# First layer norm of three segments applied to the input's turned copy, with its scales and offsets spread through DRAM

## The chip, the cores and the metric

The kernel runs on one core of one Trainium2 chip. A core has TensorE (PE in the profile; PEld its weight loads), VectorE (DVE), ScalarE (ACT), GpSimd (POOL) and SyncE (SP), each with an instruction queue of its own, and 16 DMA engines that move data between DRAM and the on-chip memory. The metric is the device time of one execution in microseconds; the median of the runs counts.

## The reference

The input x has 2048 tokens of 1024 channels. One block of attention with a compressive memory and one MLP follow each other, both behind a layer norm without weights:

```python
def _layernorm(x, axis=-1, eps=1e-5):
    m = jnp.mean(x, axis=axis, keepdims=True)
    v = jnp.var(x, axis=axis, keepdims=True)
    return (x - m) / jnp.sqrt(v + eps)

# _A_ref(x, wq, wk, wv, wo, beta): H = 32 heads of Dh = 32, N = 4 segments of L = 512 tokens
#   q, k, v = x @ wq, x @ wk, x @ wv, cut into heads and segments
#   for each segment s:
#     p = softmax(q k^T / sqrt(Dh) + causal mask);  a_dot = p v
#     a_mem = (phi(q) M) / (phi(q) z + 1e-6);  phi(t) = t + 1 for t > 0, exp(t) otherwise
#     o = g a_mem + (1 - g) a_dot;  M += phi(k)^T v;  z += sum phi(k)
#   return o @ wo
h = x + _A_ref(_layernorm(x), A_wq, A_wk, A_wv, A_wo, A_beta)
h2 = h + (gelu(_layernorm(h) @ w1 + b1) @ w2 + b2)      # d_ff = 3584
```

## The kernel before

The tokens are worked off in two halves of 1024 (`HT`), each of two segments of 512 tokens. A segment is named (half, sl), with sl 0 or 1. A half passes through attention, the output projection, the second layer norm and the first MLP product ("mixer pairs", 14 in a half); the second MLP product closes the kernel. Float32 precision is reached on TensorE with split operands: each operand is held as a high part and a low part, and `mm3` issues three products (high by high, high by low, low by high).

**What the first norm has to deliver.** The projections need the normalised segment turned, with channels on the partitions: `yh` and `yl`, high and low part, of 8 blocks of 128 channels by 512 tokens. Before the change every segment but the very first goes through `ln1`: four tiles of 128 tokens by 1024 channels are loaded (`xt`). VectorE takes the statistics of each (`bn_stats` L134, `bn_aggr` L138). GpSimd makes the scale and the offset, one number for each token and so for each partition (L141, L142, L147). ACT normalises the tile (L182). `ln_transpose` then turns it with TensorE, in two groups of four transposes of 128x128 (L161) into one PSUM bank; ACT copies the bank out as the high part (L163), and VectorE subtracts that for the low part (L165). A segment has 8 such groups. Segment (0,0) is done by `opening`, which the change leaves alone.

**Where the norms run.** `ln1` is a generator, which its caller advances step by step between other work:
- Segment (0,1) is normalised inside the attention of half 0, during units 0 and 1. A unit is a group of four heads in one segment, and has 24 steps; a step is one `mm3` of a projection (k, q, v: `kps`, `qps`, `vps`) and what `at(step, ...)` has put on it. A variable `acc` grows by 0.7 at each step, and each time it reaches 1 the generator is advanced once.
- Segment (1,0) is normalised during the last nine mixer pairs of half 0, by `interleave(pairs, norms, 0.17)`: 0.17 steps of the norm for each step of the pairs. The tiles of (1,1) are loaded there too.
- The rest of segment (1,1), `acts["ahead"]`, is done in units 0 and 1 of half 1, at 0.55 for each step.

**What sets the order.** The recorded instructions stand in program order on each engine; an engine takes its own queue in order and waits at the head of it. SyncE starts nearly all DMAs. A unit's products reach attention through it: a projection is corrected on VectorE (`side` and `kk`, `qq`, L443), and SyncE copies its rows in three DMAs for each of four groups into `ks` and `qs` (L420). TensorE then forms scores `pqk` from them (L563), VectorE reduces these with the mask (L565), ACT takes the exponential sum (L567, `junk`), and a score block frees the PSUM buffer for another. Weights for the next group of heads are loaded by SyncE (`wr`, L682) and split by VectorE (L689) and GpSimd (L693, four pieces for each weight). In unit 0 of each half GpSimd also writes the mask and a pattern `pat` (L341 to L357), which VectorE casts into `ks` (L676).

Of the kernel before, what the change touches and what calls it, by code (L numbers as in the profile page):

```python
# [10 lines left out]
F32 = mybir.dt.float32  # L11
F32R = mybir.dt.float32r
AF = mybir.ActivationFunctionType
ALU = mybir.AluOpType
# [3 lines left out]
P = 128  # L18
S = 2048
D = 1024  # L20
# [7 lines left out]
HT = 1024  # L28
# [12 lines left out]
EPS = 1e-5  # L41
# [6 lines left out]
def raw(ap):  # L48
    return ap.bitcast(F32)


def build(tc, x, wq, wk, wv, wo, beta, w1, b1, w2, b2, out):
# [16 lines left out]
    mhalf = const.tile([P, 1], F32, name="mhalf")  # L69
# [27 lines left out]
    acts = {}  # L97
# [107 lines left out]
    def chain(*gens):  # L205
        for g in gens:
            yield from g
# [6 lines left out]
    def ln1(half, sl, delay=0, aside=None, gap=1):  # L214
        xs = []
        for t in range(4):
            xt = lnp.tile([P, D], F32, tag="ln", name="xt", bufs=4)
            r0 = half * HT + (4 * sl + t) * P
            nc.sync.dma_start(xt, x[0, r0:r0 + P, :])
            xs.append(xt)  # L220
        for _ in range(delay):
            yield

        def home():
            if ("y", half, sl) not in acts:
                acts["y", half, sl] = acts["y", sl] = seg_tiles(sl, "y")
            return acts["y", sl]

        yield from ln_tiles(lnp, xs, None, None, False, act=True, aside=aside, gap=gap,
                            fold=lambda src, t4: ln_transpose(src, *home(), t4, ("av", "pt", "pt"), slow=True))  # L230

    def opening():

# [129 lines left out]
    def attention(half, first):  # L363
# [343 lines left out]
            at(6, partial(wsplit, 0, "v", "scalar", 6))  # L707
        for m, f in first.pop("rest").items() if first else ():
            at(m, f)
        side = acts.pop("ahead") if half else ln1(0, 1, 3, gap=2)  # L710
        if first:
            next(side)
        for n in range(16):
            u = unit(n)
            heads(u, 24 * n)
            g, sl = ORDER[n]
# [26 lines left out]
            acc = 0.0  # L743
            for c in range(24):
                name = "kqv"[c // 8]
# [685 lines left out]

    for half in range(2):
        acts["zt"] = zt = tc.alloc_tile_pool(name=f"zt{half}", bufs=1, side="right")
        attention_pool(half)
        first = None if half else opening()
        if half:
# [11 lines left out]
        if half == 0:  # L1448
            nc.sync.dma_start(mz_dram, acts["mz"])
        ab.release()  # L1450
        zx = acts["zx"] = tc.alloc_tile_pool(name=f"zx{half}", bufs=1, side="right", reuse_waits="tile")
        mq = tc.alloc_tile_pool(name=f"mq{half}", bufs=1, side="right", reuse_waits="tile")
        pp = tc.alloc_tile_pool(name=f"post{half}", bufs=1, reuse_waits="tile")
# [93 lines left out]
    top.close()  # L1547


_INS = ["A_x", "A_wq", "A_wk", "A_wv", "A_wo", "A_beta", "B_w1", "B_b1", "B_w2", "B_b2"]  # L1550


# [16 lines left out]
```

## Time and profile before

| | |
|---|---|
| median of the runs | 2188.95 us (3 runs, 2188.53 to 2190.12) |
| profiled execution | 2189.65 us, its span 2187.9 us |
| mean granted TensorE clock | 0.999 |
| TensorE busy | 2159.1 us, 99% of the span |
| VectorE, ACT, GpSimd busy | 1363.0, 1100.8, 949.9 us |
| transposes of the first norm by `ln_transpose` | 96, the first at 32.1 us, the last at 878.5 us |

All rows of the prediction come from this profiled execution. A row of a timeline has the start in us, the duration in us, the engine, the line, the operation, what it writes and reads, the shape, and in brackets the idle time of the engine just before and what ended it. A row of the stretches has the window, its length, the busy time (and number of instructions) of PE, PEld, DVE, ACT and POOL, the granted clock, the DMA share and GB/s. A row of grouped instructions has the line, the operation, the count, and smallest, median and largest duration in ns. A row of DMA issues has the count, the size of each and the median time from issue to landing.

### The profile page before, as it was taken

Reading aid. Unit: us, or ns where it says so; the run is one execution under the profiler, and the core shown is the slowest. Engines: PE = TensorE matmul, PEld = TensorE weight load, DVE = VectorE, ACT = ScalarE, POOL = GpSimd, SP = SyncE. Lnnn points to the kernel's source line nnn. Section 1 sums busy time; section 2 is a strip of 40 time slices with the busy share of each in tenths; the row PEclk is TensorE's granted clock in tenths of the full one; section 3 lists DMA queues with packets and bytes.
Section 4 is the critical chain, followed back from the end, with each engine's and each line's share of the span. In section 5 each row is a group of like instructions: output and inputs, shape, how many; then the busy total and the mean of one; then the engine's idle time right before and its main releaser. Section 6 shows DMA issues by size and latency. Waiting matters only on the chain.

```text
span 2187.9 us, 33209 instructions
## 1 busy us (share of the span) xinstructions
PE 2159.1 (99%) x10937; PEld 1750.7 (80%) x10937; DVE 1363.0 (62%) x2696; ACT 1100.8 (50%) x2433; POOL 949.9 (43%) x1206
## 2 busy tenths in 40 slices
PE   7999999999999999999999999999999999999999
PEld 6777777778888887877777768888887888888887
DVE  6766666665745656766667655745666765577653
ACT  5777777762543445777777652643443232323221
POOL 5533335562444434433335561534445544256330
PEclk9999999999999999999999999999999999999999
DMA  6544445664575655544444664575569775576762
GB/s 181 136 107 106 106 106 136 192 199 164 156 209 155 183 163 138 139 108 108 107 108 131 197 192 147 173 217 161 171 189 378 270 231 187 190 245 229 247 223 92
DMA packets 352405, 376.20 MB, mean 172 GB/s; under 512 B 27214, under 2 KB 244330, under 8 KB 352234
## 3 DMA queue, kind: packets, MB, share of 16 engines
q1 hardware_dynamic: 288778, 336.98, 50.8%
q10 hardware_dynamic: 63456, 37.10, 5.6%
q8 instruction: 87, 1.43, 0.3%
q14 instruction: 84, 0.69, 0.1%
HBM read 241.27 MB, written 82.38 MB: 148 GB/s over the span
## 4 chain that ended last, share of the span: by engine, by line
PE 89%; DMA 4%; DVE 3%; ACT 1%; POOL 1%; issue 1%; SPq 0%; ACTq 0%; DVEq 0%; POOLq 0%
PE po L1405 22%; PE bps L1009 10%; PE cps L1009 7%; PE dps L1009 6%; PE pst L613 3%; PE po L627 3%; PE pqk L563 3%; PE kps L127 3%; PE pwo L127 3%; PE kps L128 3%; PE qps L127 2%; PE kps L129 2%; PE pwo L129 2%; PE pwo L128 2%; PE qps L128 2%; PE qps L129 2%
## 5 line engine op out<-in xcount | busy, mean ns | idle before, releaser
L565 DVE CUSTOM_DVE_ANT_0 pqk<-pqk,mask 128x512 f32<-128x512 f32 (+2 forms) x384 | 216.9, 565 | 241.3 <-PE pqk L563 214.8
L567 ACT ACTIVATE junk<-pqk,mx 128x512 f32<-128x512 f32 (+2 forms) x384 | 225.1, 586 | 137.1 <-DVE mx L565 130.5
L620 POOL TENSOR_SCALAR_AFFINE_SELECT e<-e 128x128 f32<-128x128 f32 (+1 forms) x384 | 136.2, 356 | 268.3 <-ACT e L616 254.5
L693 POOL TENSOR_TENSOR wl<-wr,wh 128x256 fp32r<-128x256 f32 x268 | 198.5, 756 | 112.1 <-PE pqk L563 88.1
L616 ACT ACTIVATE e<-pst 128x384 f32<-128x384 f32 (+1 forms) x384 | 200.3, 528 | 72.3 <-PE pst L613 70.3
L1415 DVE TENSOR_TENSOR c<-c,po 128x512 f32<-128x512 f32 x160 | 105.4, 683 | 152.4 <-PE po L1405 149.6
L563 PE MATMUL pqk<-ks,qs 96*128 96x512 f32 (+2 forms) x384 | 138.8, 362 | 7.1 <-DMA qs<-qq 4.3
L613 PE MATMUL pst<-qs,ks 104*128 104x512 f32 (+3 forms) x512 | 140.9, 318 | 1.0 <-ACT e L616 0.4
L613 PEld LDWEIGHTS pst<-qs,ks 104*128 104x128 f32 x512 | 95.7, 188 | 34.7 <-ACT e L616 10.7
L1405 PE MATMUL po<-w2h,zh 128*128 128x512 f32 x378 | 121.0, 390 | 0.7 <-DVE zh L1345 0.4
L1262 POOL TENSOR_TENSOR w2r<-w2r 128x512 f32<-128x512 f32 x54 | 85.9, 1603 | 73.7 <-DMA w2r<-in_B_w 50.0
L127 PE MATMUL qps<-yh,wh 128*128 128x512 f32 x256 | 113.8, 444 | 0.0
L127 PE MATMUL kps<-yh,wh 128*128 128x512 f32 (+1 forms) x264 | 113.0, 428 | 0.0
L1009 PE MATMUL bps<-zh,sb 128*128 128x512 f32 x336 | 111.1, 391 | 0.0
L1009 PE MATMUL bps<-zh,sa 128*128 128x512 f32 x336 | 110.8, 390 | 0.0
L1121 POOL TENSOR_TENSOR s<-r 128x512 f32<-128x512 f32 x28 | 44.1, 1575 | 143.4 <-DVE sa L1137 84.9
L127 PE MATMUL vps<-yh,wh 128*128 128x512 f32 x256 | 105.0, 410 | 0.0
L1405 PE MATMUL po<-w2h,hl 128*128 128x512 f32 x322 | 103.1, 390 | 0.4 <-DVE hl L1345 0.3
L128 PE MATMUL kps<-yl,wh 128*128 128x512 f32 (+1 forms) x264 | 102.4, 388 | 0.9 <-DVE yl L289 0.5
L129 PE MATMUL kps<-yh,wl 128*128 128x512 f32 (+1 forms) x264 | 101.8, 386 | 0.0
L128 PE MATMUL qps<-yl,wh 128*128 128x512 f32 x256 | 101.4, 396 | 0.0
L129 PE MATMUL qps<-yh,wl 128*128 128x512 f32 x256 | 101.0, 394 | 0.0
(271 smaller groups left out, 6211.1 us busy)
## 6 DMA issues: line engine op xcount, KB each, us to landing
hr<-h_dram SPq DMA_DIRECT2D x112, 448.0 KB, 5.4
w2r<-in_B_w SPq DMA_DIRECT2D x122, 256.0 KB, 4.4
r<-in_B_w SPq DMA_DIRECT2D x56, 512.0 KB, 4.7
ks<-kk SPq DMA_DIRECT2D x360, 64.0 KB, 2.0
qs<-qq SPq DMA_DIRECT2D x360, 64.0 KB, 2.0
h_dram<-ht ACTq DMA_DIRECT2D x84, 256.0 KB, 3.7
wx<-in_B_w SPq DMA_DIRECT2D x56, 256.0 KB, 3.5
o_dram<-side SPq DMA_DIRECT2D x52, 256.0 KB, 3.9
```

Of the source, the lines that this page charges most:

```text
L127: nc.tensor.matmul(ps, ah, bh, start=first, stop=False)
L128: nc.tensor.matmul(ps, ah, bl, start=False, stop=False)
L129: acts["mm"] = nc.tensor.matmul(ps, al, bh, start=False, stop=last)
L563: nc.tensor.matmul(ps, u["qs"][0:96, j, i * P:(i + 1) * P], u["ks"][0:96, j, 0:n], start=True, stop=True)
L565: nc.vector.tensor_tensor_reduce(out=ps, in0=ps, in1=mask[:, 512 - n:512], op0=ALU.add, op1=ALU.min, scale=-SCALE, scalar=3.0e38, accum_out=m)
L567: at(now[0] + 1, lambda: nc.scalar.activation(acts["junk"][:, :n], ps, AF.Exp, bias=m, scale=-1.0, accum_out=u["mx"][:, 1, i, j:j + 1]))
L613: nc.tensor.matmul(ps[:, o:o + 512 - P * jk], u["ks"][:, j, jk * P:(jk + 1) * P], u["qs"][:, j, jk * P:512], start=True, stop=True)
L616: nc.scalar.activation(e, ps[:, :w], AF.Exp, scale=SCALE)
L620: nc.gpsimd.affine_select(d, d, pattern=[[0, 2], [1, P]] if n == 2 else [[1, P]], compare_op=ALU.is_ge, fill=0.0, base=0, channel_multipli ...
L693: nc.gpsimd.tensor_tensor(l[:, c], wr[:, c], raw(h)[:, c], op=ALU.subtract)
L1009: nc.tensor.matmul(ps, x_[:, c, :], y_[:, c, :], start=first and c == 0 and n == 0, stop=last and c == 3 and n == 2, skip_group_check=True)
L1405: nc.tensor.matmul(ps, x_[:, k], y_[k], start=opens and k == 0 and i == 0, stop=closes and k == self.KP - 1 and i == 2, skip_group_check=True)
```

## The change

A second input is made on the host before the launch: `A_xT`, the transpose of x, 1024 by 2048. For the segments (0,1), (1,0) and (1,1), `ln1` is replaced by two generators.

`row_scales` still loads the four tiles of x and takes their statistics. GpSimd writes scale and offset of the tokens into one tile `rn` of 128 partitions by 8 numbers, and one DMA stores it, turned, to `rn_dram` (8 by 128).

`column_pairs` loads the segment from the turned input, in four tiles `xc` of 128 partitions by 2 by 512 (512 KB each), and loads `rn_dram` spread over all 128 partitions as `rows` (scales and offsets of 512 tokens, 512 KB in the on-chip memory). Then VectorE multiplies each `xc` by the scales, GpSimd adds the offsets, ACT copies the high part, and VectorE subtracts it for the low part, each on 128x1024. No transposes are left in these segments. The generator is advanced at 0.9 instead of 0.7 for each step in half 0, 0.23 instead of 0.17 in the mixer pairs; the 0.55 of half 1 stays. A pool for `rn` and `rows` is new. The changed kernel's lines are 1 to 65 further down than before (L443 is L502, L563 is L622, L565 is L624, L676 is L735, L689 is L748, L693 is L752).

```diff
+    rn_dram = {k: dram.tile([8, P], F32, name=f"rn_dram{k[0]}{k[1]}") for k in ((0, 1), (1, 0), (1, 1))}
...
+    def row_scales(half, sl):
+        rn = acts["rnp"].tile([P, 8], F32, name="rn", bufs=2)
+        xs = []
+        for t in range(4):
+            xt = lnp.tile([P, D], F32, tag="ln", name="xt", bufs=4)
+            r0 = half * HT + (4 * sl + t) * P
+            nc.sync.dma_start(xt, x[0, r0:r0 + P, :])
+            xs.append(xt)
+        for _ in range(3):
+            yield
+        for t in range(4):
...
+            r = rn[:, t:t + 1]
+            nc.gpsimd.tensor_scalar(v[:, 0:1], mv[:, 1:2], 1.0, EPS, op0=ALU.mult, op1=ALU.add)
+            nc.gpsimd.tensor_tensor(r, v[:, 0:1], mhalf, op=ALU.pow)
+            nc.gpsimd.tensor_scalar(rn[:, 4 + t:5 + t], mv[:, 0:1], -1.0, r, op0=ALU.mult, op1=ALU.mult)
+            yield
+        nc.sync.dma_start(rn_dram[half, sl].rearrange("k p -> p k"), rn)
+        yield
+
+    def column_pairs(half, sl):
+        t0 = half * HT + 512 * sl
+        ws = []
+        for c in range(4):
+            w = lnp.tile([P, 2, 512], F32, tag="ln", name="xc", bufs=4)
+            nc.sync.dma_start(w, xt_[256 * c:256 * c + 256, t0:t0 + 512].rearrange("(c p) n -> p c n", p=P))
+            ws.append(w)
+            if c % 2:
+                yield
+        rows = acts["rnp"].tile([P, 2, 512], F32, name="rows", bufs=1)
+        nc.sync.dma_start(rows.rearrange("p a n -> p (a n)"),
+                          rn_dram[half, sl].rearrange("k p -> (k p)").partition_broadcast(P))
+        for _ in range(2 if half else 3):
+            yield
+        r, nb = (rows[:, i, :].unsqueeze(1).to_broadcast([P, 2, 512]) for i in range(2))
+        home = []
+        for c in range(5):
+            if c < 4:
+                nc.vector.tensor_tensor(ws[c], ws[c], r, op=ALU.mult)
+                nc.gpsimd.tensor_tensor(ws[c], ws[c], nb, op=ALU.add)
+                yield
+            if c > 0:
...
+                home.append(nc.scalar.copy(yh[:, k, :], ws[c - 1]))
+                yield
+                nc.vector.tensor_tensor(yl[:, k, :], ws[c - 1], raw(yh[:, k, :]), op=ALU.subtract)
+                yield
...
-        side = acts.pop("ahead") if half else ln1(0, 1, 3, gap=2)
+        side = acts.pop("ahead") if half else chain(row_scales(0, 1), column_pairs(0, 1))
...
-                    acc += 0.55 if half else 0.7
+                    acc += 0.55 if half else 0.9
...
-            acts["ahead"] = ln1(1, 1, gap=2)
+            acts["rnp"] = tc.alloc_tile_pool(name="rn1", bufs=1, reuse_waits="tile")
+            acts["ahead"] = column_pairs(1, 1)
             interleave(chain(*(mixer.pair(j) for j in range(HP - 9, HP))),
-                       chain(ln1(1, 0, 2), islice(acts["ahead"], 3)), 0.17)
+                       chain(row_scales(1, 0), column_pairs(1, 0), row_scales(1, 1), islice(acts["ahead"], 3)), 0.23)
```

How the rows now stand is shown at three places: in two queues of half 0's units 0 and 1, and in one of half 1's. First SyncE's queue in unit 0 of half 0, before:

```order
L420 DMA ks_179<-side 32x512 x6
L682 DMA wr<-in_A_wk 128x8x128
L420 DMA qs_181<-side 32x512 x3
L682 DMA wr<-in_A_wq 128x8x128
L420 DMA ks_179<-side 32x512 x3
L420 DMA qs_181<-side 32x512 x3
```

The same place after, where the six rows have become ten:

```order
L741 DMA wr<-in_A_wk 128x8x128
L256 DMA rn_dram_116<-rn 128x8x1
L265 DMA xc<-in_A_xT 128x2x512 x2
L479 DMA qs_187<-side 32x512 x3
L741 DMA wr<-in_A_wq 128x8x128
L479 DMA ks_185<-side 32x512 x3
L265 DMA xc<-in_A_xT 128x2x512 x2
L479 DMA qs_187<-side 32x512 x3
L270 DMA rows<-rn_dram_116 128x1024
L479 DMA ks_185<-side 32x512 x3
```

The store of the scales and two loads of turned tiles stand ahead of the first three `qs` copies, and the load of the rows stands between the second `qs` copies and the `ks` copies that followed them.

Second, VectorE in unit 0 of half 0, from the statistics to the reductions of the first scores, before:

```order
L676 CAST ks_179<-pat 8x2048
L385 SCALAR_TENSOR_TENSOR pk,zc<-e,r 128x512
L134 BN_STATS st<-xt 128x6 x2
L138 BN_AGGR mv<-st 128x2
L676 CAST ks_180<-pat 8x2048
L443 TENSOR_TENSOR side<-qps,side 128x512
...
L461 COPY pkf<-pkn 128x512
L565 ISA pqk,mx<-pqk,mask 128x512
L565 ISA mx 128x1
L165 TENSOR_TENSOR yl_484<-pt,yh_483 128x4x128
L498 COPY vt<-vps 128x512
L565 ISA pqk,mx<-pqk,mask 128x384
```

And after, where `side<-qps` is preceded by the statistics of all four tiles:

```order
L247 BN_STATS st<-xt 128x6 x2
L249 BN_AGGR mv<-st 128x2
L502 TENSOR_TENSOR side<-qps,side 128x512
L735 CAST identr<-ident 128x128
L748 CAST wh<-wr 128x1024
L520 COPY pkf<-pkn 128x512
L624 ISA pqk,mx<-pqk,mask 128x512
L624 ISA mx 128x1
L278 TENSOR_TENSOR xc<-xc,rows 128x1024
L557 COPY vt<-vps 128x512
L278 TENSOR_TENSOR xc<-xc,rows 128x1024
L624 ISA pqk,mx<-pqk,mask 128x384
```

The multiplication by the scales, which reads `rows`, now stands between the first reduction of scores and the second.

Third, GpSimd at the start of half 1's attention, behind the two pieces of a split weight of 128x1024, before:

```order
L104 TENSOR_TENSOR wl<-wr,wh 128x1024 x2
L141 TENSOR_SCALAR v<-mv 128x1
L142 TENSOR_TENSOR v<-v,mhalf 128x1
L147 TENSOR_SCALAR nb<-mv,v 128x1
L341 MEMSET mask 128x512
L355 MEMSET pat 8x4
L342 AFFINE_SELECT mask<-mask 128x128
L356 AFFINE_SELECT pat<-pat 8x4
L693 TENSOR_TENSOR wl<-wr,wh 128x256
L357 AFFINE_SELECT pat<-pat 8x4
```

And after:

```order
L105 TENSOR_TENSOR wl<-wr,wh 128x1024 x2
L279 TENSOR_TENSOR xc<-xc,rows 128x1024 x2
L752 TENSOR_TENSOR wl<-wr,wh 128x256 x4
L400 MEMSET mask 128x512
L414 MEMSET pat 8x4
L401 AFFINE_SELECT mask<-mask 128x128
L415 AFFINE_SELECT pat<-pat 8x4
L416 AFFINE_SELECT pat<-pat 8x4
L279 TENSOR_TENSOR xc<-xc,rows 128x1024 x2
```

Two additions of offsets on 128x1024 and four pieces of a weight now come ahead of the mask and the pattern, in place of three operations on 128x1.

More of the change, by code (lines that the diff above doesn't have):

```diff
@@ L49, in raw, with build @@
     return ap.bitcast(F32)
-def build(tc, x, wq, wk, wv, wo, beta, w1, b1, w2, b2, out):
+def build(tc, x, xt_, wq, wk, wv, wo, beta, w1, b1, w2, b2, out):
     nc = tc.nc
@@ L230, in ln1 @@
                             fold=lambda src, t4: ln_transpose(src, *home(), t4, ("av", "pt", "pt"), slow=True))
+    def row_scales(half, sl):
[9 more added lines that the diff above has]
+        for t in range(4):
+            st = lnp.tile([P, 2, 6], F32, name="st", bufs=3)
+            for i in range(2):
+                nc.vector.bn_stats(st[:, i, :], xs[t][:, 512 * i:512 * i + 512])
+            mv = lnp.tile([P, 2], F32, name="mv", bufs=3)
+            nc.vector.bn_aggr(mv, st)
+            v = lnp.tile([P, 2], F32, name="v", bufs=3)
+            r = rn[:, t:t + 1]
[5 more added lines that the diff above has]
+        yield
@@ new lines, in column_pairs @@
+    def column_pairs(half, sl):
[20 more added lines that the diff above has]
+            if c > 0:
+                if not home:
+                    acts["y", half, sl] = acts["y", sl] = seg_tiles(sl, "y")
+                yh, yl = acts["y", sl]
+                k = slice(2 * c - 2, 2 * c)
+                home.append(nc.scalar.copy(yh[:, k, :], ws[c - 1]))
+                yield
+                nc.vector.tensor_tensor(yl[:, k, :], ws[c - 1], raw(yh[:, k, :]), op=ALU.subtract)
+                yield
@@ L1433, in build @@
         acts["zt"] = zt = tc.alloc_tile_pool(name=f"zt{half}", bufs=1, side="right")
+        if half == 0:
+            acts["rnp"] = tc.alloc_tile_pool(name="rn0", bufs=1)
         attention_pool(half)
@@ L1450, in build @@
         ab.release()
+        if "rnp" in acts:
+            acts.pop("rnp").release()
         zx = acts["zx"] = tc.alloc_tile_pool(name=f"zx{half}", bufs=1, side="right", reuse_waits="tile")
@@ L1559 @@
     arrays, args = {}, []
+    inputs = {**inputs, "A_xT": np.asarray(inputs["A_x"])[0].T}
     for name in _INS:
```

2 lines of the change are left out of this document (1 added, 1 removed).

## The prediction

> **What bounds the kernel now.** I read the busy times and the chain of work that ended last first, then the table of stretches around the three places where the norms run, then TensorE's timeline there.
>
> ```profile
> PE 2159.1 (99%) x10937; PEld 1750.7 (80%) x10937; DVE 1363.0 (62%) x2696; ACT 1100.8 (50%) x2433; POOL 949.9 (43%) x1206
> PE 89%; DMA 4%; DVE 3%; ACT 1%; POOL 1%; issue 1%; SPq 0%; ACTq 0%; DVEq 0%; POOLq 0%
> 31.00:47.00 16.00, 14.46 (x75) 11.48 (x74) 11.23 (x28) 9.65 (x19) 9.04 (x16) 1.00 0.62 164
> 47.00:52.00 5.00, 4.35 (x16) 3.85 (x17) 3.35 (x13) 4.08 (x15) 3.23 (x6) 0.66 0.02 6
> 780.00:836.00 56.00, 55.12 (x252) 45.31 (x250) 29.85 (x45) 23.11 (x35) 16.62 (x16) 1.00 0.50 146
> 860.00:885.00 25.00, 23.71 (x126) 18.92 (x125) 20.43 (x60) 16.00 (x44) 12.71 (x21) 1.00 0.52 138
> ```
>
> TensorE is busy 99% of the span and holds 89% of the chain, so each matmul removed shortens the kernel, and each wait put before a matmul lengthens it. The stretches (busy PE, PEld, DVE, ACT, POOL, then the granted clock, DMA share and GB/s) show three settings. In half 0's units 0 and 1 (A, 22 to 66 us: segment (0,1)), PE works 14.46 of 16 us and then shows a stretch at a clock of .66. In the mixer pairs (B, 713 to 836: segment (1,0)) it is nearly full, 55.12 of 56. In half 1's first units (C, from 836: segment (1,1)) it stands idle for 1.29 of the last 25 us. What waits at A has to be found in the order of the queues, since there PE works from products that have just been made.
>
> **Gain: the transposes.**
>
> ```profile
> L161 PE MATMUL pt<-ident,xt x96: 270/272/422, 32.1 to 878.5; 128*128 128x128 f32 x96
> 32.13 0.66 PE L161 MATMUL pt<-ident,xt 128*128 128x128 f32 x4 [1.05 <-ACT xt L182]
> 34.47 0.39 PE L563 MATMUL pqk<-ks,qs 96*128 96x512 f32 x1
> 35.39 0.60 PE L161 MATMUL pt<-ident,xt 128*128 128x128 f32 x4
> 35.74 0.48 PE L127 MATMUL kps<-yh,wh 128*128 128x512 f32 x1
> 36.06 0.40 PE L128 MATMUL kps<-yl,wh 128*128 128x512 f32 x1
> 36.29 0.40 PE L129 MATMUL kps<-yh,wl 128*128 128x512 f32 x1
> ...
> 48.26 1.06 PE L161 MATMUL pt<-ident,xt 128*128 128x128 f32 x4
> 64.21 0.60 PE L161 MATMUL pt<-ident,xt 128*128 128x128 f32 x4
> 65.76 0.50 PE L128 MATMUL kps<-yl,wh 128*128 128x512 f32 x1 [0.35 <-DVE yl L165]
> 811.40 0.47 PE L1009 MATMUL dps<-zh,sa 128*128 128x512 f32 x1 [0.88 <-DVE ht L1033]
> ```
>
> The 96 transposes run in 24 groups of four. From a group's start to the second matmul behind it is 36.06 − 35.39 = .67 us; a plain step is .23 (36.06 to 36.29). A group therefore costs .44, all 24 cost 10.6 us, 3.5 for the eight of each segment. Two waits are for the transposed path: 1.05 at 32.13 and .35 at 65.76. The .88 at 811.40 is not of this path but of VectorE's load, and I leave it in. ACT is relieved of the twelve normalisations and of the copies out of PSUM; I count nothing for it, because elsewhere in these stretches PE waits for it rarely, and what it does at A is paced by VectorE below.
>
> **Cost at A: first the scales.** The new `row_scales` computes the statistics of four tiles, three small GpSimd operations for each, and one store that only the fourth tile releases.
>
> ```profile
> 22.87 0.69 DVE L443 TENSOR_TENSOR side<-kps,side 128x512 fp32r<-128x512 f32 x1 [3.13 <-ACT side L437]
> 25.66 1.39 DVE L385 SCALAR_TENSOR_TENSOR pk<-e,r 128x512 f32<-128x512 f32 x1 [0.84 <-ACT r L448]
> 26.98 1.28 DVE L134 BATCH_NORM_STATS2 st<-xt 128x6 f32<-128x512 f32 x2
> 28.29 0.21 DVE L138 BATCH_NORM_AGGREGATE mv<-st 128x2 f32<-128x12 f32 x1
> 28.53 1.23 DVE L676 CAST ks<-pat 8x2048 fp32r<-8x2048 f32 x1
> 40.54 0.19 POOL L141 TENSOR_SCALAR v<-mv 128x1 f32<-128x1 f32 x1 [0.91 <-DVE mv L138]
> 41.47 0.27 POOL L147 TENSOR_SCALAR nb<-mv,v 128x1 f32<-128x1 f32 x1
> ```
>
> On VectorE the order after is: side(kps), cast, tile 0, pk, tile 1, cast, tiles 2 and 3. From 23.56: two casts 2.46, four tiles at 1.28 + .21 = 6.0, pk 1.3, together 33.3; less than .3 of it overlaps. Three GpSimd operations, 40.54 to 41.74, are 1.2. The scales are ready at about 34.3.
>
> **Then SyncE's queue.** The store of the scales stands ahead of two 512 KB loads and of the first three `qs` copies, which in the order before came straight behind the wk load.
>
> ```profile
> 26.73 0.53 SPq L682 DMA_DIRECT2D wr<-in_A_wk  x1
> 28.33 2.68 SPq L420 DMA_DIRECT2D qs<-side  x3
> 39.26 1.85 SPq L420 DMA_DIRECT2D qs<-side  x3
> wr<-in_A_wk SPq DMA_DIRECT2D x3, 512.0 KB, 3.9
> qs<-side SPq DMA_DIRECT2D x9, 64.0 KB, 2.0
> q1 hardware_dynamic: 288778, 336.98, 50.8%
> ```
>
> Issue times are .53 for a large load and 1.85/3 = .62 for a copy. Store at 34.3, two loads, two copies: the third `qs` issues at 37.1 and lands 2.0 later, 39.1 at the earliest, where before it was issued by 31.0. PE, without the 1.05 and the one group, would want its first pqk at 34.47 − 1.05 − .44 = 33.0. It waits 6 us there; that is the lower bound, since the copies also stand behind 1 MB of loads and the store's pieces.
>
> The store writes 128 × 8 floats transposed, 1024 pieces of 4 bytes. All packets of queue q1 took 50.8% of 16 × 2187.9 us, so 61.6 ns of engine time each; 64 pieces on each engine are 3.9 us, with 2.0 for landing 5.9. Landed by about 40.2, it is behind other work, because the queue reaches the load of the rows only later: from 37.7 come wr 0.53, three ks 1.86, two loads 1.06, three qs 1.86, so 43.0 at the earliest. That load spreads 4 KB over 128 partitions, 512 KB written; nearest row 3.9 us. The rows stand in SBUF at **R ≥ 46.9**. The upper bound takes the delays of the first wait back into the queue (later qs copies need PE's later products, up to 6 us) and 1 us for the longer transfers: 54. I take R = 49, nearer the lower end, since most of what the queue needs is computed by then.
>
> The Trainium skill (DMA: Bandwidth & Descriptors, Specifications) has transfers under 512 B done by read-modify-write, and under Bandwidth counts some 10.5 ns for a packet. By that count the pieces would take .7 us, not 3.9, an estimate that would shift the copies behind them some 3 us earlier and leave the total near +8. No run here shows a 4-byte store alone.
>
> **Then VectorE stands at the rows.** Behind the first pqk's reduce VectorE's next instruction is the multiplication that waits for R; the rest of unit 0's reductions is queued behind it, and so PE's pqk buffers.
>
> ```profile
> 39.59 0.40 PE L563 MATMUL pqk<-ks,qs 96*128 96x512 f32 x1
> 47.65 0.50 PE L563 MATMUL pqk<-ks,qs 96*128 96x512 f32 x1 [1.02 <-ACT junk L567]
> L921 DVE TENSOR_TENSOR hb<-ht,b2c x16: 1170/1208/1227, 510.9 to 1379.7; 128x1024 f32<-128x1024 f32 x16
> L103 ACT CAST zh<-wr x8: 1046/1048/1052, 496.7 to 1323.1; 128x1024 fp32r<-128x1024 f32 x8
> 835.42 2.40 POOL L104 TENSOR_TENSOR wl<-wr,wh 128x1024 fp32r<-128x1024 f32 x1 [0.37 <-ACT wh L103]
> L693 POOL TENSOR_TENSOR wl<-wr,wh 128x256 fp32r<-128x256 f32 x22 | 15.6, 734 | 8.4 <-DVE wh L689 7.4 <-PE pqk L563 0.9
> ```
>
> A multiplication is 1.21, a GpSimd addition 2.40, a copy on ACT 1.05. From R: mult, vt .69, mult, reduce .71, ACT .78: the fourth pqk (39.59 before) comes at R + 4.6 = 53.6. On GpSimd, mult 1.2, add 2.4, wl .73, add 2.4, three wl 2.2 and a third add 2.4 come to R + 11.3; copy, subtraction and the reductions queued behind that subtraction on VectorE bring the third pqk block (47.65 before) to R + 14 to 15.5, about 63. That is 15.5 late. Five of the segment's groups, from that at 48.26 to that at 64.21, lay behind this point and give back 2.2, and the .35 at 65.76 goes: **A = +13**, 9 at R = 46.9 with the shorter tail, 18 at R = 54. Savings ahead of the waits only lengthen the waits.
>
> The waits also touch the clock: behind the 1.02 at 47.65 the stretch 47 to 52 has .66. That price is already in the time before; a second such stretch would add some 1.7 (5 × .34) and lies inside the upper end. The Trainium skill (TensorE: Matmul & The Clock Gate, Part 1) lets PE fall to half clock after about 3.4 us idle and need as long to recover. The row has it after a shorter wait; by the rule each of two 6 us waits would cost about 1.7, an estimate.
>
> **B.** Here the paced steps are spread over nine pairs in 123 us, 13.7 us a pair, and the rows' load stands about one pair ahead of the multiplication that needs it, several times the 3.9 us of its landing: VectorE finds them there. GpSimd gets four additions, 9.6 us, where it works 16.62 of 56; each can put off the pair's own GpSimd work by some 2.4 to 3.7 us, and at 16.62 of 56 it has that to spare before PE asks. VectorE takes four multiplications and four subtractions at 1.21 in place of eight subtractions of half the size: some 4 us more in a stretch where it works 29.85 of 56. SyncE loads the segment twice, 2 MB turned besides 2 MB of x for the statistics, with the DMA share at .50. I cost all of that at nothing; were a cover gone, the price is one wait of the kind at 811.40, .88. Eight groups go: **−3.5**; −4.4 if that .88 goes as well, −2.6 if a second comes.
>
> **C.** GpSimd's queue now holds two additions (4.8 us) ahead of the mask, the pattern `pat`, and four wl.
>
> ```profile
> 843.28 0.19 POOL L357 TENSOR_SCALAR_AFFINE_SELECT pat<-pat 8x4 f32<-8x4 f32 x1
> 844.98 1.78 DVE L676 CAST ks<-pat 8x2048 fp32r<-8x2048 f32 x1
> 851.40 0.64 DVE L443 TENSOR_TENSOR side<-qps,side 128x512 fp32r<-128x512 f32 x1
> 854.31 0.47 PE L563 MATMUL pqk<-ks,qs 96*128 96x512 f32 x1 [0.16 <-DMA qs<-side]
> ```
>
> After 837.8: additions to 842.6, four wl at .73 are 2.9, and the pattern's small operations, of which the last is quoted, about 1.4: `pat` stands at 846.9 and the cast starts 1.9 later than before. VectorE then has two subtractions and a multiplication (3.6) and pk, cast ahead of side(qps), in place of statistics: it ends 854.4 instead of 852.04, `qs` lands at 856.6, and PE, three groups ahead, would want it at 854.31 − .16 − 1.3 = 852.8. It waits 3.8 there, and against the time before stands at +2.3; the multiplications between the reductions make it up to 1.9 more one block on, +4.2. Four later groups give back 1.8, and of the 1.29 of waits from 860 to 885 I take .9 as absorbed: **+1.5**, from −3.5 (the additions hidden) to +4.2 (nothing given back).
>
> **Sum.** +13 − 3.5 + 1.5 = +11 on the profiled execution's 2189.65 (span 2187.9 and 1.75 around it): 2200.65. That execution lies .7 above the median of the runs, so 2200.0 in their terms.
>
> **Rivals.**
> - *Rows in time; only the savings remain: faster.* For: PE is 99% busy, 24 groups are 10.6, the two waits 1.4. It decides at R. With B at −3.5 and C at −3.5 the kernel breaks even at A = +7, six under the forecast, so R at about 43; with C at +1.5, at A = +2 and R at 38. Against it: SyncE's issue times alone reach 46.9. It comes true if the statistics or the queue are ahead of my addition by that much, or if PE's order lets the later steps run while VectorE waits. All savings and no new wait give 2188.95 − 12.0 = 2177; half of the way there, 2183.
> - *Within .2%.* R at the lower end, the short tail (+9), and C wholly saved (−3.5): 9 − 3.5 − 3.5 = +2, 2191.
> - *Much slower.* The store's pieces hold the copies, R about 56: A = +20, and 2189 + 20 − 3.5 + 4.2 = 2210. For: 1024 pieces stand against the 32 rows of a `qs` copy; against: 5.9 us are hidden behind the queue.
>
> **Chances.** .52 for the forecast (its own range 2194 to 2207: A 9 to 18, C −3.5 to +4.2, without the corners), .12 for much slower, .18 for within .2%, .18 for faster. About .2%, 4.4 us, is what a measurement of this kernel can tell from no change. Slower therefore has .64. The range 2183 to 2210 leaves out most of the faster case and the top of the slowest.
>
> **What would show it.** The transposes' 96 matmuls gone, PE busy some 10 us less; two new waits of PE at 33 to 39 and 40 to 60 us, the second ended by VectorE behind its first multiplication, whose own wait ends with the rows' DMA at 47 to 54; the units' clock below 1.00 there. B's matmuls end 3.5 us earlier against its start; `pat`'s cast at about 847 plus the lag. I am wrong if the rows' load issues before 40 us, if the copies land ahead of the store, or if PE fills the wait with other units' work.

## The result: 65 us slower, at all three places

The changed kernel takes 2254.53 us (median of 6 runs, 2252.64 to 2256.44); the kernel before, on the same chip, 2189.53 (2186.61 to 2195.41). The ratio is 1.0296, 95% interval 1.0284 to 1.0308. The forecast was 2200.0, range 2183 to 2210: the sign was right, the size was not.

The page's busy times and chain of the changed kernel, whose profiled span is 2254.5 us:

```profile
PE 2163.8 (96%) x10841; PEld 1749.7 (78%) x10841; DVE 1378.9 (61%) x2696; ACT 1086.6 (48%) x2409; POOL 996.3 (44%) x1218
PE 85%; DMA 5%; DVE 4%; POOL 2%; issue 2%; ACT 1%; SPq 1%; ACTq 0%; POOLq 0%; DVEq 0%
```

The 96 transposes are gone, yet TensorE is busy 5 us longer and stands idle for some 90 us instead of 29. GpSimd's busy time grew by 46 us, though twelve additions of 2.4 us make only 29. The table of stretches, at A:

```profile
31.00:47.00 16.00, 2.86 (x15) 2.05 (x13) 5.15 (x11) 0.00 (x0) 5.73 (x12) 0.68 0.31 24
47.00:60.00 13.00, 6.27 (x21) 5.02 (x21) 0.76 (x2) 0.78 (x2) 0.00 (x0) 0.61 1.00 276
60.00:80.00 20.00, 8.52 (x33) 5.83 (x31) 17.55 (x21) 7.08 (x15) 16.98 (x9) 0.83 0.16 44
80.00:100.00 20.00, 13.99 (x52) 10.86 (x52) 12.53 (x29) 8.55 (x27) 13.41 (x16) 0.83 0.43 116
```

TensorE does 2.86 us in the 16 in which it did 14.46 before. The DMA engines are busy for 31% of that stretch and move 24 GB/s, where they moved 164 before. From 60 to 80 VectorE and GpSimd are nearly full (17.6 and 17.0 of 20 us), and TensorE's granted clock is below 1 in all four stretches.

To place the loss I take three marks in TensorE's timeline of every run: the start of the 25th scores matmul (88.90 before), of half 1's first `kps` (836.45) and of half 1's 14th scores matmul (883.27). A is the lateness at the first against the kernel before, B what is added up to the second, C up to the third. "Against before" is against the runs of before on the same chip. The marks come from one profiled execution of each kernel, the times from the median of its runs: A, B and C together differ from the whole by up to 5 us.

| kernel | ratio, 95% interval | against before | A | B | C |
|---|---|---|---|---|---|
| changed | 1.0296 (1.0284 to 1.0308) | +65.0 | +37.7 | +25.2 | +6.6 |
| (0,1) only | 1.0171 (1.0156 to 1.0186) | +37.6 | +39.6 | −0.8 | −0.6 |
| (1,0), (1,1) only | 1.0137 (1.0120 to 1.0154) | +30.4 | +0.7 | +20.8 | +8.0 |
| before + loose 4-byte stores | 1.0050 (1.0035 to 1.0065) | +10.5 | +9.4 | +0.5 | +0.6 |
| 32-byte pieces | 1.0179 (1.0164 to 1.0194) | +39.8 | +28.4 | +2.8 | +7.1 |
| rows from x, no store | 1.0144 (1.0123 to 1.0166) | +32.9 | +23.9 | −0.2 | +7.9 |
| rows from x, additions on VectorE | 1.0160 (1.0141 to 1.0179) | +37.0 | +25.0 | +6.2 | +4.5 |
| rows from x, loaded early | 1.0122 (1.0102 to 1.0142) | +26.4 | +18.4 | +2.5 | +7.7 |
| TensorE spreads | 1.0132 (1.0110 to 1.0153) | +30.8 | +15.7 | +7.4 | +7.9 |
| late loads | 1.0121 (1.0100 to 1.0141) | +29.1 | +17.2 | +8.3 | +8.6 |
| slow statistics | 1.0148 (1.0131 to 1.0165) | +32.4 | +16.0 | +9.9 | +8.8 |
| early statistics | 1.0138 (1.0120 to 1.0157) | +31.1 | +19.2 | +3.7 | +7.3 |
| chain apart | 1.0133 (1.0110 to 1.0155) | +28.9 | +16.6 | +4.1 | +7.8 |
| without additions | 1.0057 (1.0042 to 1.0072) | +11.9 | +8.7 | +1.0 | +3.6 |
| without additions and multiplications | 1.0021 (1.0012 to 1.0030) | +4.4 | +7.9 | −1.6 | +0.6 |
| (1,0) only, chain apart | 1.0014 (1.0003 to 1.0025) | +3.0 | −0.6 | +2.3 | −0.7 |

### The profile page after: what moved, and what is told of

Its sections match the earlier page's. It is cut to its first block, busy times and chain, and to the rows that moved or that the text cites. A ratio compares the mean times of both kernels' runs of the same rounds, so it can differ in the third digit from the quotient of the medians.

```text
span 2254.5 us, 33042 instructions
## 1 busy us (share of the span) xinstructions
PE 2163.8 (96%) x10841; PEld 1749.7 (78%) x10841; DVE 1378.9 (61%) x2696; ACT 1086.6 (48%) x2409; POOL 996.3 (44%) x1218
## 4 chain that ended last, share of the span: by engine, by line
PE 85%; DMA 5%; DVE 4%; POOL 2%; issue 2%; ACT 1%; SPq 1%; ACTq 0%; POOLq 0%; DVEq 0%
PE po L1464 22%; PE bps L1068 8%; PE cps L1068 7%; PE dps L1068 5%; PE pst L672 3%; PE po L686 3%; PE pqk L622 3%; PE kps L128 3%; PE kps L130 3%; PE kps L129 3%; PE qps L128 2%; PE pwo L128 2%; PE pwo L130 2%; PE pwo L129 2%; PE vps L128 2%; PE qps L130 2%
## 5 line engine op out<-in xcount | busy, mean ns | idle before, releaser
L624 DVE CUSTOM_DVE_ANT_0 pqk<-pqk,mask 128x512 f32<-128x512 f32 (+2 forms) x384 | 216.9, 565 | 272.3 <-PE pqk L622 245.9
L752 POOL TENSOR_TENSOR wl<-wr,wh 128x256 fp32r<-128x256 f32 x268 | 210.7, 802 | 106.9 <-PE pqk L622 80.9
L622 PE MATMUL pqk<-ks,qs 96*128 96x512 f32 (+2 forms) x384 | 140.1, 365 | 48.0 <-DMA qs<-side 24.9
L622 PEld LDWEIGHTS pqk<-ks,qs 96*128 96x128 f32 x384 | 73.3, 191 | 69.4 <-issue 35.1
L672 PEld LDWEIGHTS pst<-qs,ks 104*128 104x128 f32 x512 | 95.7, 188 | 34.5 <-ACT e L675 10.6
```

The costliest lines, as they stand in the source:

```text
L622: nc.tensor.matmul(ps, u["qs"][0:96, j, i * P:(i + 1) * P], u["ks"][0:96, j, 0:n], start=True, stop=True)
L624: nc.vector.tensor_tensor_reduce(out=ps, in0=ps, in1=mask[:, 512 - n:512], op0=ALU.add, op1=ALU.min, scale=-SCALE, scalar=3.0e38, accum_out=m)
L672: nc.tensor.matmul(ps[:, o:o + 512 - P * jk], u["ks"][:, j, jk * P:(jk + 1) * P], u["qs"][:, j, jk * P:512], start=True, stop=True)
L752: nc.gpsimd.tensor_tensor(l[:, c], wr[:, c], raw(h)[:, c], op=ALU.subtract)
```

## The experiments: where the loss lies

**Only (0,1), and only half 1's segments.** The undone part goes back to `ln1`:

```diff
-                       chain(row_scales(1, 0), column_pairs(1, 0), row_scales(1, 1), islice(acts["ahead"], 3)), 0.23)
+                       chain(ln1(1, 0, 2), islice(acts["ahead"], 3)), 0.17)      # (0,1) only
...
-        side = acts.pop("ahead") if half else chain(row_scales(0, 1), column_pairs(0, 1))
+        side = acts.pop("ahead") if half else ln1(0, 1, 3, gap=2)                   # half 1 only
```

> Only segment (0,1) is changed; (1,0) and (1,1) go through ln1 as before. Additive theory (each place pays for itself): the first matmuls of scores lose 37 us by 100 us of the span, nothing is given back, so 2189 + 37 = 2226. Rival (what is lost at unit 0 is absorbed later, and the loss belongs to the pairs and half 1): under 2200.

> Only segments (1,0) and (1,1) are changed; (0,1) goes through ln1. Additive theory: the other 29 us of the 66, about 2218, with the waits of the pairs on sb and u (8.6 and 8.2 us) still there. Rival: these waits come from the attention of half 0 having ended later, then they vanish and the time is 2185 to 2195.

+37.6 and +30.4, together 68 against 65: each place's loss stays when the other is undone. Of the 39.6 us lost at A only 1.4 are given back by the third mark.

**The pieces.** In the changed kernel, DMA issues from 30 to 62 us (count, size, median us to landing), SyncE's timeline, and the first matmuls behind the wait:

```profile
xc<-in_A_xT SPq DMA_DIRECT2D x4, 512.0 KB, 10.1
qs<-side SPq DMA_DIRECT2D x9, 64.0 KB, 5.9
wr<-in_A_wq SPq DMA_DIRECT2D x1, 512.0 KB, 13.9
...
rn_dram<-rn SPq DMA_DIRECT2D x1, 4.0 KB, 10.2
```

```profile
36.13 0.39 SPq L256 DMA_DIRECT2D rn_dram<-rn  x1
36.61 1.04 SPq L265 DMA_DIRECT2D xc<-in_A_xT  x2
37.75 3.68 SPq L479 DMA_DIRECT2D qs<-side  x3
...
55.93 0.58 SPq L270 DMA_DIRECT2D rows<-rn_dram  x1
```

```profile
53.73 0.77 PE L622 MATMUL pqk<-ks,qs 96*128 96x512 f32 x1 [19.87 <-DMA qs<-side]
54.30 0.63 PE L128 MATMUL vps<-yh,wh 128*128 128x512 f32 x1
54.72 0.63 PE L129 MATMUL vps<-yl,wh 128*128 128x512 f32 x1
...
57.18 0.42 PE L128 MATMUL kps<-yh,wh 128*128 128x512 f32 x1
57.44 0.40 PE L129 MATMUL kps<-yl,wh 128*128 128x512 f32 x1
```

4 KB take 10.2 us to land, and the transfers issued behind them are late with them: a weight of 512 KB 13.9 us, where it took 4.8 in the kernel before. The DMA packets, from 37 to 38 us and then from 38 to 46:

```profile
DMA packets 1040, 0.00 MB, mean 4 GB/s; under 512 B 1040, under 2 KB 1040, under 8 KB 1040
q1 hardware_dynamic: 1040, 0.00, 47.3%
...
DMA packets 92, 0.18 MB, mean 23 GB/s; under 512 B 2, under 2 KB 2, under 8 KB 92
q1 hardware_dynamic: 92, 0.18, 41.8%
```

The small packets are all recorded within one microsecond. In the eight that follow, until the store lands at 46.4, only 92 packets pass, at 23 GB/s. The profile shows that what stands behind the store crawls, but not what holds it.

Two kernels take the store apart. One adds the stores to the kernel before, where nothing waits for them:

```diff
+                nc.sync.dma_start(rn_dram[k].rearrange("k p -> p k"), ident[:, 0:8])   # in ln1, after the first tile's statistics
```

> The kernel before, with ln1 everywhere, plus three stores of 128x8 constants turned to 8x128, 1024 pieces of 4 bytes each, in SyncE's queue where the changed kernel has its stores; nothing waits for them and they wait for nothing. Pieces theory (the 4-byte writes hold the DMA engines for some 10 us, and every transfer behind them lands that much later): a landing of 8 to 12 us for the store, the qs copies behind it late, and the time 5 to 35 us above before. Queue theory (the damage is SyncE waiting for the scales with copies behind it, and VectorE waiting for the rows): within 3 us of before.

The other keeps the changed kernel, with bigger pieces:

```diff
-        nc.sync.dma_start(rn_dram[half, sl].rearrange("k p -> p k"), rn)
+        nc.sync.dma_start(rn_dram[half, sl], rn)                              # rn_dram is [P, 8]
```

> The changed kernel with the scales stored as they lie, 128 pieces of 32 bytes in place of 1024 of 4, in the same place of the queue and with the same waits; the rows then hold scales and offsets in another order and another size (the variance is multiplied by 400), so that part of the computation is not the reference's. Pieces theory: the store lands in 2 to 3 us, PE's first wait for qs falls from 19.9 to 6 to 8 us, the loss at unit 0 from 37 to about 13 us, the whole to 2195 to 2212. Queue theory: within 5 us of 2254.

The stores' rows in these two, and the first waits with 32-byte pieces:

```profile
rn_dram<-ident SPq DMA_DIRECT2D x3, 4.0 KB, 12.4
```

```profile
rn_dram<-rn SPq DMA_DIRECT2D x3, 4.0 KB, 1.4
```

```profile
44.63 0.77 PE L622 MATMUL pqk<-ks,qs 96*128 96x512 f32 x1 [10.33 <-DMA qs<-side]
59.54 0.79 PE L622 MATMUL pqk<-ks,qs 96*128 96x512 f32 x1 [8.64 <-ACT junk L626]
```

The loose stores alone cost 10.5 us, 9.4 of them at A, where copies for the first scores stand right behind: the queue theory's "within 3 us" falls. In the pairs they cost .5, though a 512 KB load issued right behind one of them took 15.6 us to land: there no matmul waited for it. With 32-byte pieces the changed kernel is 25.2 us faster by the runs (65.0 − 39.8), 30.2 by the two profiled spans (2254.5 and 2224.3). By the marks it gains 9.3 at A and 22.4 in B.

How the pieces cost so much in B, where the loose stores cost almost nothing, shows in the changed kernel's VectorE timeline and in its chain of work that ended last:

```profile
801.36 1.23 DVE L278 TENSOR_TENSOR xc<-xc,rows 128x1024 f32<-128x1024 f32 x1 [7.05 <-DMA rows<-rn_dram]
...
887.32 2.36 DVE L278 TENSOR_TENSOR xc<-xc,rows 128x1024 f32<-128x1024 f32 x2 [7.08 <-DMA rows<-rn_dram]
```

```profile
792.83 8.44 DMA rows<-rn_dram
...
864.27 12.85 DMA rn_dram<-rn
877.18 10.12 DMA rows<-rn_dram
```

VectorE stood at the rows twice in B, with the pairs' own work queued behind it, and TensorE's two longest waits there, 8.57 and 8.24 us, ended at 805.06 and 891.03. With 32-byte pieces the first of VectorE's two waits is 3.23 and the second is gone. The pieces theory holds for 25 us, but PE's first wait fell to 10.33, not to 6 to 8, and its 2195 to 2212 did not come: 40 us are left.

**The waits.** Next the scales are waited for by nothing: rows come from a row of x.

```diff
-        nc.sync.dma_start(rn_dram[half, sl].rearrange("k p -> p k"), rn)
...
-                          rn_dram[half, sl].rearrange("k p -> (k p)").partition_broadcast(P))
+                          x[0, t0, :].partition_broadcast(P))
```

> The changed kernel without the stores of the scales; rows is loaded in the same place of the queue from a row of x instead, so nothing waits for the scales, and the norm is computed with other numbers. Waits theory (what is left of the loss without the 4-byte pieces, some 38 us, is SyncE standing at the store and VectorE at the rows): 2176 to 2190, PE's first wait for qs under 4 us. Arithmetic theory (the multiplications, additions and copies on VectorE, GpSimd and ACT, which block one another, cost it): 2200 or more.

```diff
-                nc.gpsimd.tensor_tensor(ws[c], ws[c], nb, op=ALU.add)
+                nc.vector.tensor_tensor(ws[c], ws[c], nb, op=ALU.add)
```

> The same, with the additions of the offsets on VectorE instead of GpSimd. In the changed kernel a multiplication of 1.23 us took 2.98 where GpSimd's addition ran, and a GpSimd piece of .73 took 1.71. If the two engines exclude each other there and that is on the path, this is 3 to 8 us faster than the kernel with the additions on GpSimd, and VectorE's multiplications all take 1.2. If not, it is 2 to 6 us slower, because VectorE has 12 x 1.2 us more to do.

In a third kernel the same load stands at the head of `column_pairs`:

> As the kernel with rows from x and no stores (2221), but rows is loaded ahead of the turned tiles instead of behind ten copies and loads; again the norm is computed with other numbers. If VectorE standing at rows with the scores' reductions queued behind it (9.3 us there) is the main part of the loss at unit 0, that wait goes to under 2 us and the time falls by 7 to 11, to 2210 to 2214. If the sequence multiply, add, copy, subtract over three engines is the main part, it falls by less than 4.

VectorE's timeline, first with rows from x, then with rows loaded early:

```profile
49.47 1.23 DVE L277 TENSOR_TENSOR xc<-xc,rows 128x1024 f32<-128x1024 f32 x1 [9.34 <-DMA rows<-in_A_x]
```

```profile
42.41 1.22 DVE L277 TENSOR_TENSOR xc<-xc,rows 128x1024 f32<-128x1024 f32 x1
43.55 0.68 DVE L556 COPY vt<-vps 128x512 f32<-128x512 f32 x1
44.15 3.02 DVE L277 TENSOR_TENSOR xc<-xc,rows 128x1024 f32<-128x1024 f32 x1
```

Taking the scales' wait out of SyncE's queue is worth 6.9 us (39.8 to 32.9), taking VectorE's wait for rows out 6.5 more. The second is just under the 7 to 11 expected, and neither theory's number is met: the 9.3 us wait ended, but the larger part of A stayed at 18.4. The waits theory's 2176 to 2190 is wrong (PE's first wait was 4.38), and "2200 or more" is right. With the additions on VectorE the kernel is 4.1 us slower, as the second branch of its expectation said; at C it is 3.4 better, in the pairs 6.4 worse, and at A nothing is gained, so VectorE has no more room there than GpSimd. Most of its multiplications took 1.2, but not all: up to 1.75 in half 0's first units, and up to 2.3 in the pairs, beside GpSimd's work there.

**Spreading without DRAM.** TensorE turns the scales; then loads, statistics and subtraction are moved.

```diff
+            nc.vector.tensor_copy(bc, rn[:, 4 * i:4 * i + 4].unsqueeze(2).to_broadcast([P, 4, P]))
+            for t in range(4):
+                nc.tensor.transpose(pb[:, t * P:(t + 1) * P], bc[:, t, :], ident)
+            nc.scalar.copy(rows[:, i, :], pb)
```

> The changed kernel with the scales and offsets spread by TensorE instead of DRAM: VectorE copies them to 128 columns each (two 128x512 copies a segment), eight transposes of 128x128 in two groups turn them, ACT copies them to rows. Computes the reference. 6 of the 24 groups come back, 2.6 us. Waits theory: no wait for rows, PE's first wait for qs 3 to 5 us, since 1 MB of turned tiles still stands ahead of the qs copies; 2178 to 2192. Arithmetic theory: 2200 or more.

> The same with the loads of the turned tiles of segment (0,1) two steps later, so that SyncE issues them behind the first six qs copies instead of ahead of them. If the copies' place behind 1 MB is what delays the first scores, 3 to 5 us faster than with the loads ahead, 2174 to 2188; else the same within 1.5.

> The kernel with TensorE's spreading and late loads (2217), paced at 0.6 in unit 0 and 1.1 behind it instead of 0.9: one tile's statistics fewer stand ahead of side(qps) on VectorE. Computes the reference. If the statistics' place makes the first scores late, they come 1 to 2 us earlier, and the time is 2213 to 2216; if it is worth nothing, within 1.5 of 2217, and a crowding of additions in unit 1 would make it slower.

> As the kernel with TensorE's spreading and late loads (2217), with two of the three empty steps ahead of the statistics taken out: statistics, scales and multiplications a step or two earlier. It is the control for the next kernel: within 3 us of 2217 if the scales are no longer what is waited for, 4 to 8 us faster if they are.

```diff
-        for c in range(5):                    # copy and subtraction of block c - 1
+        for c in range(6):                    # copy of block c - 1, subtraction of block c - 2
```

> As the control, with the subtraction of a block put one block later on VectorE, behind the next multiplication, so that it doesn't wait there for GpSimd's addition and ACT's copy. If the in-order sequence over three engines is what holds VectorE and the scores behind it, 4 to 10 us faster than the control; if the engines' work itself (GpSimd and VectorE excluding each other) is, within 3 us of it.

All five lie at +29 to +32, "2200 or more". The later loads are worth 1.7, and the earlier statistics cost 2.0; both lie inside the intervals. With slow statistics the first scores came at 34.22 (34.47 before), some 4 us earlier than with late loads (38.12); the statistics ahead of side(qps) do make them late. But A was 16.0 against 17.2, and the whole 3.3 us slower, inside the intervals: the gain at the first scores was gone again by the 25th, and the 2213 to 2216 did not come. The later subtraction is worth 2.2 against its control, "within 3". That speaks for the work and against the order of the sequence, but with intervals of some 5 us to each side it doesn't exclude a gain of 4.

**The work.** From "chain apart" the additions are taken away, then the multiplications:

```diff
-                nc.gpsimd.tensor_tensor(ws[c], ws[c], nb, op=ALU.add)
...
-                nc.vector.tensor_tensor(ws[c], ws[c], r, op=ALU.mult)                # second kernel only
```

> The kernel with the later subtraction (2217) without GpSimd's twelve additions of the offsets; the norm then lacks its mean. If GpSimd's load in units 0 and 1 of each half and in the pairs, and its exclusion with VectorE, are what is left of the loss, the weight pieces take .73 again and the time falls to 2188 to 2200. If VectorE's multiplications and subtractions, or the place of the statistics, are, it stays above 2208.

> The same without VectorE's twelve multiplications either; the turned input is split into high and low part as it is. Against the kernel without additions this shows the multiplications alone: under 4 us if VectorE has room for 1.2 us each, 5 to 12 us if each of them holds up the scores' reductions behind it. What is left above 2180 then belongs to statistics, spreading by TensorE, loads, and the copies and subtractions.

VectorE's and GpSimd's groups from 30 to 100 us, with the additions ("chain apart"), and without them:

```profile
L288 DVE TENSOR_TENSOR xc<-xc,rows 128x1024 f32<-128x1024 f32 x4 | 8.7, 2187 | 0.0
L759 DVE CAST wh<-wr 128x1024 fp32r<-128x1024 f32 x7 | 7.2, 1030 | 3.5 <-DMA wr<-in_A_wq 3.2 <-DMA wr<-in_A_wv 0.3
L763 POOL TENSOR_TENSOR wl<-wr,wh 128x256 fp32r<-128x256 f32 x28 | 26.7, 979 | 8.1 <-DVE wh L759 8.1
L289 POOL TENSOR_TENSOR xc<-xc,rows 128x1024 f32<-128x1024 f32 x4 | 10.9, 2730 | 1.2 <-DVE xc L288 1.2
```

```profile
L288 DVE TENSOR_TENSOR xc<-xc,rows 128x1024 f32<-128x1024 f32 x4 | 5.7, 1431 | 0.0
L758 DVE CAST wh<-wr 128x1024 fp32r<-128x1024 f32 x8 | 5.5, 689 | 2.7 <-DMA wr<-in_A_wv 1.5 <-DMA wr<-in_A_wq 1.2
L762 POOL TENSOR_TENSOR wl<-wr,wh 128x256 fp32r<-128x256 f32 x32 | 29.0, 930 | 13.7 <-DVE wh L758 13.7
```

The twelve additions are worth 17.0 us (28.9 to 11.9, with intervals of 5 and 3 us to each side), the twelve multiplications 7.5 more, a little over half a microsecond each; the second lies in "5 to 12". The time without additions, 2200.48, is just above the 2188 to 2200 expected. VectorE's casts returned to .69, but the mean of the weight pieces only to .93, with single ones up to 1.72 beside VectorE's two-input multiplications and subtractions, which are still there; that half of the expectation was wrong. At A, 8 us stay with both gone, and 3.5 of them are there at the first scores already (38.00 against 34.47). Statistics, copies, subtractions of 1.46 us, spreading and loads are what is left; they were not separated.

**(1,0) alone**, in the pairs, with everything above:

> Only segment (1,0), in the mixer pairs, is changed, with TensorE's spreading and the later subtraction; (0,1) and (1,1) go through ln1. It computes the reference. 6 groups of transposes are saved, 2.6 us. If the pairs have the room on VectorE and GpSimd, 2184 to 2187 against 2188; if the additions and multiplications hold the pairs' own u and sb, as with all three segments changed, 2190 to 2200.

+3.0 us, interval +.7 to +5.5: no gain, though 6 groups are saved; 2190.88 is at the lower end of the second theory's 2190 to 2200. No version tried beats the kernel before.

## Why the forecast was wrong

By the marks A was 37.7 instead of 13, B 25.2 instead of −3.5, and C 6.6 instead of 1.5.

**Right:** the sign of the whole, of A and of C; that SyncE's queue holds the first copies behind the scales; that VectorE stands at the rows at A. The scales were forecast for 34.3, the store issued at 36.13. The price of a group cannot be read off, because TensorE waits wherever it was saved.

**The store's price.** The step that failed is "64 pieces on each engine are 3.9 us, with 2.0 for landing 5.9 ... it is behind other work". The 61.6 ns were the mean over all packets of the queue, and on that page only 27214 of 352405 packets are under 512 bytes. Landing took 10.2 us, so by the same division (10.2 − 2.0)/64 = .128 us for a piece. The small packets passed within 1 us, so time on the engines was the wrong measure of a landing, whichever price is taken. And the store hid behind nothing: the loads behind it landed after 10.1 (median of the turned tiles) and 13.9 us (the weight) instead of 4 to 5. The pieces are 25 of the 54 missing microseconds. Why 4-byte pieces land so slowly stays open. The Trainium skill (DMA: Bandwidth & Descriptors, Bandwidth) led the other way: its 10.5 ns a packet, which it gives for loads, made +8. The trace has no more than that for the packets' passing (1040 on 16 engines in 47.3% of 1 us are 7 ns each), but twelve times that for the landing, divided by pieces. The same page's read-modify-write below 512 bytes (Specifications) would fit the slowness of 4-byte pieces, but not that 32-byte ones landed in 1.4 us.

**B.** Two steps failed here. "VectorE finds them there" did not hold: VectorE waited 7 us for the rows at both places, against 3.23 at one of them with 32-byte pieces. And "I cost all of that at nothing" did not hold either: where −3.5 was forecast for the eight groups saved, B is +2.8 with 32-byte pieces, −.2 with rows from x and +2.3 with (1,0) alone. Without additions and multiplications it is −1.6.

**VectorE and GpSimd exclude each other.** This step was missing in A's sum: "A multiplication is 1.21, a GpSimd addition 2.40", each as if alone. In the changed kernel they ran side by side:

```profile
61.71 1.23 DVE L278 TENSOR_TENSOR xc<-xc,rows 128x1024 f32<-128x1024 f32 x1 [6.42 <-DMA rows<-rn_dram]
...
63.45 2.98 DVE L278 TENSOR_TENSOR xc<-xc,rows 128x1024 f32<-128x1024 f32 x1
```

```profile
63.02 2.34 POOL L279 TENSOR_TENSOR xc<-xc,rows 128x1024 f32<-128x1024 f32 x1 [24.87 <-DVE xc L278]
65.31 1.71 POOL L752 TENSOR_TENSOR wl<-wr,wh 128x256 fp32r<-128x256 f32 x1
```

VectorE's second multiplication starts at 63.45 but lasts until the addition has ended (65.36) and 1.07 more. GpSimd's weight piece, .73 alone, starts at 65.31 and ends .6 after that multiplication (66.43): each seems to wait for the whole of the other. The same shows in the means of "chain apart" above, 979 and 1030 ns for pieces and casts, against 734 and 687 in the kernel before. The Trainium skill states this (SBUF — State Buffer, Who interferes with whom): a VectorE instruction with two inputs in the on-chip memory contends with a GpSimd instruction that reads it, and the port pair that they share is an exclusive lock. The trace agrees. In `ln1` the subtraction read PSUM and the scaling ran on ACT; the new path has eight two-input VectorE instructions for each segment. The weight pieces from 30 to 100 us before and after, and `ln1`'s subtractions before (smallest, median and largest duration in ns), show that the old path stretched neither:

```profile
L693 POOL TENSOR_TENSOR wl<-wr,wh x36: 722/734/742, 33.6 to 99.6; 128x256 fp32r<-128x256 f32 x36
L752 POOL TENSOR_TENSOR wl<-wr,wh x20: 722/738/1783, 36.1 to 96.9; 128x256 fp32r<-128x256 f32 x20
L165 DVE TENSOR_TENSOR yl<-pt,yh x24: 678/685/693, 35.5 to 880.7; 128x512 fp32r<-128x512 f32 x24
```

Which part of the additions' 17 us is the lock and which GpSimd's own 2.4 us was not separated. The kernel with the additions on VectorE speaks against the lock alone: no addition runs on GpSimd there, no multiplication in half 0's first units takes more than 1.75, and A is 25.0 all the same.

**From R to the scores.** R was forecast at 49, with bounds of 46.9 and 54. It was 61.7 in the changed kernel, 53.46 with 32-byte pieces and 49.47 without a store: the queue's share lay inside the bounds, and the pieces added some 8 us. Behind it, "R + 4.6" was R + 6.1 (67.79), and "R + 14 to 15.5" was R + 18.8:

```profile
67.79 0.79 PE L622 MATMUL pqk<-ks,qs 96*128 96x512 f32 x1 [7.51 <-ACT junk L626]
...
80.50 0.51 PE L622 MATMUL pqk<-ks,qs 96*128 96x512 f32 x1 [2.89 <-ACT junk L626]
...
86.91 0.44 PE L622 MATMUL pqk<-ks,qs 96*128 96x384 f32 x1 [2.71 <-ACT junk L626]
...
100.12 0.47 PE L622 MATMUL pqk<-ks,qs 96*128 96x512 f32 x1 [2.93 <-DMA qs<-qq]
```

Then "give back 2.2" for five groups failed in sign: the lateness grew from 32.9 at 80.50 to 37.7. The first 2.2 us of it came with the wait that ended at 86.91. Ahead of it VectorE's cast and subtraction stood beside GpSimd's last two additions:

```profile
76.25 2.51 DVE L748 CAST wh<-wr 128x1024 fp32r<-128x1024 f32 x1
79.32 3.44 DVE L288 TENSOR_TENSOR yl<-xc,yh 128x1024 fp32r<-128x1024 f32 x1
```

```profile
74.86 3.34 POOL L279 TENSOR_TENSOR xc<-xc,rows 128x1024 f32<-128x1024 f32 x1
79.31 2.36 POOL L279 TENSOR_TENSOR xc<-xc,rows 128x1024 f32<-128x1024 f32 x1
```

The rest came with slow steps of TensorE and with the wait at 100.12.

**The clock.** One stretch of 1.7 was allowed for. Between 24 and 112 us 28 steps of plain matmuls took .40 to .47 us, most of them .43, instead of .23. That is 5.6 us more in all, against .9 in the kernel before. Steps of double length count as busy time, and TensorE was busy 4.7 us longer where some 10 us less had been forecast. After the wait that ended at 53.73 the fast steps return at 57.18, 3.5 us on. The Trainium skill (TensorE: Matmul & The Clock Gate, Part 1) gives some 3.4 us of work for recovery, and the trace agrees.

**C.** The order was read rightly: in the changed kernel GpSimd's two additions and four pieces stand ahead of the pattern. The first scores were late by 3.4 more than half 1's start was (62.9 to 66.3), where the forecast had 2.3. What failed is "Four later groups give back 1.8" and the .9 taken "as absorbed": C grew to 6.6. Without the additions it is 3.6, without the multiplications too .6.

**The rivals.** Much slower was the nearest and was given .12, with R at 56 and +21. Its mechanism, that the pieces hold the copies, is what came, but it counted them at A alone, and its 2210 is 44 us below the result. The condition of the rival "rows in time" was met in the kernels with rows from x early and TensorE's spreading, and they still lost 26 to 32 us. My break-even in R left out the work behind R.

## What to carry to other kernels

Moving work off the busiest engine gains only what the others can take within the stage: here 10.6 us of TensorE were traded for instructions on VectorE and GpSimd at a place where both paced the scores, and these cost some 24 us even in a kernel that no longer waited for the scales through DRAM (28.9 to 4.4). A price from a row holds for the neighbours that it had in that row: two instructions that each ran at 1.2 and 2.4 us may run one after the other when they meet. Before a store that turns a small tile, count its pieces, and look at who waits for the transfers behind it, not only at who waits for the store.

## What the runs showed that I had not expected

- A store of 4 KB in 1024 pieces of 4 bytes landed in 9.2 to 15.3 us (nine stores in four kernels), and the transfers behind it were late by about as much; in 128 pieces of 32 bytes it landed in 1.4 to 2.1.
- VectorE's cast of the pattern, 1.22 us, took 3.31 beside GpSimd's addition (2.72) in half 1's first unit: a one-input instruction was stretched too.
